# Unit products chained through PSUM, more output rows by seven products, and an order played from a timetable, in a float32 kernel of attention and gated FFN

## The chip, the cores and the metric

The kernel runs on one core of one Trainium2 chip. The time is device microseconds of that core, the median of several runs; a profiled execution gives the rows that are read here.

## The reference

Input x is 2048 x 512. Two branches are mixed row by row with a gate from x:

```python
def reference(A_x, A_wqkv, A_wo, B_x, B_w_gate, B_w_up, B_w_down, gate_w):
    x = A_x
    g = sigmoid((x * gate_w).sum(-1, keepdims=True))
    # A: linear attention, 32 heads of 16, phi(t) = where(t > 0, t + 1, exp(t)) + 1e-6
    q, k, v = heads(x @ A_wqkv)                      # 512 x 1536
    kv = einsum("bhsd,bhse->bhde", phi(k), v); z = phi(k).sum(s)
    a = (phi(q) @ kv / (phi(q) . z + 1e-6)) @ A_wo   # 512 x 512
    # B: bilinear FFN, F = 1792
    b = ((x @ B_w_gate) * (x @ B_w_up)) @ B_w_down   # 512 x 1792, 1792 x 512
    return g * a + (1 - g) * b
```

## The kernel before

Every product is made in float32 as three matmuls of rounded parts: a matrix is split into a high part (a ScalarE copy that rounds) and a low part (a VectorE subtraction), and high x high, high x low and low x high are added in PSUM (`mm3`). A matmul is 128 x 128 weights by 512 columns.

**Phase 1** (`xop`, `k_mm`, `g_unit`) goes over 16 tiles of 128 rows: k = x W_k, phi of it, and the sums g = phi(k)^T x in four PSUM banks (`accs`); the tile's matmuls of k run up to four tiles ahead of those of g. Beside it x is loaded and added in blocks for the units (`cb_load`, `x_add`), and the raw weights of the first units come in.

**Phase 2** goes twice (a pair of 512-row chunks each time, `pair` 0 and 1) through 16 units: 14 of the FFN (gate and up columns of one block f of 128) and two of attention (q columns). `order` lists the 32 units. A **unit** is a 2 x 2 block product (two weight columns by two row chunks, inner dimension halved) done with seven products of six matmuls instead of eight; x sums and weight sums go in, and PSUM banks Y, X, R, S collect them. Before, the sums between products go through VectorE: `m2` is a ScalarE copy of Y, R = X - m2, t = R + cross0, S = t - X, and at the end the two multiplications of gate by up (`hidden`).

The raw weights of a unit (`wr`, seven blocks of 128 KB in two buffers) come as a load of three blocks on SP's queue, two ScalarE copies and one accumulating transfer of five blocks on GpSimd's queue (`w_load`, `w_add`); `w_high` and `w_low` split them into `wch` and `wcl` (two buffers).

**Down jobs** turn the units' results into output rows. A plain pair of rows is `down_jobs`: eight jobs of two rows, one PSUM bank each (`pdn`). `seven` does groups of pairs by seven products over four banks (`sa`, `sb`), with weights made of loads and accumulating transfers (`ws`, from `in_wdn`, `wrow` and their negatives `dminus`, `wminus`). Twelve of the 18 row pairs are done so, in groups of two: FIRST_SEVEN (four pairs in the first half) and SEVEN (eight in the second).

The order of everything is written by hand: `later(n, place, fn)` hangs work at a place of a unit, `do` runs it, FIRST and SECOND say after which product how many down jobs follow (`down`), and `advance` starts ScalarE, VectorE and weight steps of jobs ahead by leads. Buffers of phase 2 are 58 slots of 128 x 512 (`Buf`, `NS`). All engines and queues keep program order (`pin`). Output of the first half goes out on GpSimd's queue, of the second on SP's.

Of the kernel before, what the change touches and what calls it, by code (L numbers as in the profile page):

```python
# [31 lines left out]
LEAD_X = 4  # L32
LEAD_W = 17
GAP_L = 6
GAP_A = 14
HB = 8
FIRST_SEVEN = (((4, 5), (6, 7)), (('a', 0), (8, 9)))
FIRST_AT = (4, 8)
MINUS_AT = (1, 2, 3)
XAT = (11, 6, 4, 8, 11, 7, 11, 13, 13, 13, 10, 13)  # L40
WUNIT = (8, 5, 2)
FIRST = (
    (3, 1, 3, 0), (0, 3, 2, 1), (0, 0, 1, 1), (2, 0, 1, 0), (0, 1, 0, 2), (0, 0, 0, 1), (1, 2, 0, 2), (0, 3, 0, 0),
    (0, 0, 2, 2), (0, 2, 3, 1), (2, 1, 1, 1), (3, 2, 0, 2), (2, 0, 1, 0), (3, 3, 3, 3), (1, 2, 0, 0), (3, 0, 2, 3),
)
PLACES = "high low e m c d t s r end".split()
ATT = ((0, 8, 5, 4, 6, 4, 5, 3), (0, 5, 12, 5, 0, 9, 4, 13))
NS = 58
SECOND = (
    (2, 1, 1, 0), (0, 0, 1, 3), (2, 1, 0, 3), (1, 0, 0, 0), (0, 1, 0, 2), (0, 0, 1, 2), (2, 0, 0, 2), (0, 2, 0, 1),  # L50
    (0, 2, 1, 2), (2, 2, 2, 0), (0, 0, 2, 1), (0, 3, 3, 1), (0, 3, 1, 0), (2, 2, 0, 1), (3, 0, 2, 3), (3, 1, 0, 2),
)
STARTS = (0, 4, 4, 10)
MOST = (2, 2, 2, 2)
MOST_0 = (1, 1, 2, 2)
LEAD_X0 = 4
LEADS_0 = (15, 7, 12)
RELOAD = ((0, 1), (0, 2), (3, 4), (5, 6))
Q_AFTER = ((5, 9), (0, 3))

SLOT = {3: 0, 4: 1, 2: 2, 5: 3, 1: 4, 6: 5, 7: 6}
# [3 lines left out]
def gated_mix(ctx: ExitStack, tc, xt, xp, x, wqkv, wq, wq_add, wo, wgu, wgu_add, wdn, gate_w, out):  # L71
# [39 lines left out]
    def dma_add(dst, src):  # L111
# [17 lines left out]
    own = {i: [const.tile([P, 2, CH], F32R, name=f"xc{i}{v}") for v in "hl"] for i in (1, 4, 6)}  # L129
    xc = {2: [v[:, 0:2] for v in xa], 7: [v[:, 2:4] for v in xa],  # L130
          3: [v[:, 0:2] for v in xb], 5: [v[:, 2:4] for v in xb], **own}


    zeros = own[1][0][:, 0, 0:CH // 2].bitcast(mybir.dt.bfloat16)
# [9 lines left out]
    xsum = {i: dram.tile([P, 2, CH], F32, name=f"xsum{i}") for i in (1, 5, 6, 7)}  # L144
# [28 lines left out]
    def w_add(n):  # L173

        if n < len(order):
            _, kind, m = order[n]
# [4 lines left out]
    PARTS = ((0, 2), (2, 4), (4, 7))  # L181
# [7 lines left out]
    def w_low(n, part):  # L189
        if n < len(order):  # L190
# [5 lines left out]
    SUMS = {1: (A1, B2, 0), 3: (B1, B2, 1), 4: (A2, A1, 1), 6: (A1, B1, 0), 7: (A2, B2, 0), 2: (None, A1, 0),  # L196
            5: (None, B2, 0)}

    def x_load(tile_, pair, i, ks):
        dma(tile_, xp[pair, SUMS[i][1]][:, ks])  # L200

    def x_add(tile_, pair, i, ks):
        one, _, sub = SUMS[i]
        if sub:
            act(tile_, tile_, scale=-1.0)
        if one is not None:
            dma_add(tile_, xp[pair, one][:, ks])
# [4 lines left out]
    with tc.tile_pool(name="p1", bufs=2, reuse_waits="tile") as p1:  # L212

        warm = psum.tile([P, CH], F32, tag="Y", name="warm")
        for _ in range(WARM):
            mm(warm, zeros[:, :P], zeros, start=True, stop=True)
        gw = p1.tile([P, D], F32, name="gw", bufs=1)
        zacc = p1.tile([P, D], F32, name="zacc", bufs=1)
        nc.vector.memset(zacc, 0.0)
        wkh = p1.tile([P, KT, D], F32R, name="wkh", bufs=1)  # L220
# [7 lines left out]

        raw_of = [p1.tile([P, D], F32, tag="raw", name="wraw", bufs=4) for _ in range(KT)]
# [39 lines left out]
        def phi_k(t, pk):  # L269

            e = p1.tile([P, D], F32, tag="e", name="e")
            r = p1.tile([P, D], F32, tag="u", name="r")
            act(e, pk, AF.Exp)
            act(r, pk, AF.Relu)
            ph = p1.tile([P, D], F32, tag="ph", name="ph")
            stt(ph, e, 1.0, r, ALU.min, ALU.add)
            return t, ph

        def phi_split(t, ph):
            pkh = p1.tile([P, D], F32R, tag="pkh", name="pkh", bufs=4)  # L280
            pkl = p1.tile([P, D], F32R, tag="pkl", name="pkl", bufs=4)
            act(pkh, ph, AF.Identity, bias=epsc)
            stt(pkl, ph, EPS, pkh.bitcast(F32), ALU.add, ALU.subtract)
            stt(zacc, ph, EPS, zacc, ALU.add, ALU.add)
            pks[t] = (pkh, pkl)

        def split_x(t):
            raw = xs.pop(t)
            xnh = p1.tile([P, D], F32R, tag="xnh", name="xnh")
            xnl = p1.tile([P, D], F32R, tag="xnl", name="xnl")  # L290
            split(xnh, xnl, raw)
            junk = p1.tile([P, D], F32, tag="junk", name="junk", bufs=1)
# [47 lines left out]
        def cb_load(i):  # L340
            cbs[i] = p1.tile([P, 2, CH], F32, tag="cbs", name="cbs", bufs=3)
            x_load(cbs[i], 0, i, slice(0, 2))

        for t, i in zip((6, 7, 9, 10, 12), (4, 1, 6, 7, 3)):
            plan(t, lambda i=i: cb_load(i))
            plan(t + 2, lambda i=i: x_add(cbs[i], 0, i, slice(0, 2)))
            plan(t + 5, lambda i=i: split(*xc[i], cbs.pop(i)))
        for n, t in ((0, 8), (1, 11)):
            plan(t, lambda n=n: w_load(n))
            plan(t + 2, lambda n=n: w_add(n))  # L350
        plan(14, lambda: w_high(0))
        for part in range(3):
            plan(14 + part // 2, lambda part=part: w_low(0, part))
        plan(16, lambda: w_load(2))
# [36 lines left out]
    p2 = ctx.enter_context(tc.tile_pool(name="p2", bufs=1, reuse_waits="tile"))  # L391
    live = []
    spare, kept = [], {}

    class Buf:

        def __init__(self, name, rounded=False):
            self.home = rounded and bool(spare)
            one = spare.pop(0) if self.home else p2.tile([P, CH], F32R if rounded else F32, tag="s", name=name, bufs=NS)
            self.f = one.bitcast(F32) if rounded else one  # L400
            self.r = one
            if not self.home:
                live.append(self)
                assert len(live) <= NS, clock[0]

    def put(*some):
        for one in some:
            if one.home:
                spare.append(one.r)
            else:  # L410
                live.remove(one)

    def two(name):
        return [Buf(name + v, True) for v in "hl"]

    def split_buf(name, src, copy="act"):

        hi, lo = two(name)
        split(hi.r, lo.r, src, copy)
        return hi, lo  # L420


    at = {}

    def later(n, place, fn):
        at.setdefault((n, place), []).append(fn)

    def do(n, place):
        for fn in at.pop((n, place), []):
            fn()  # L430
        clock[0] += 1
        most = MOST if n >= units else MOST_0
        advance(dve=most[0], act=most[1])


    jobs, clock = [], [0]

    class Job:

        def __init__(self, mms, chains=(), after=None, apart=0, group=None, first=False):  # L440
            self.first, self.mms, self.after, self.apart, self.group = first, mms, after, apart, group
            self.chains = [list(c) for c in chains]
            self.free = [0] * len(self.chains)

    def always():
        return True

    def advance(**most):

        for i, job in enumerate(jobs):  # L450
            for k, chain in enumerate(job.chains):
                while chain:
                    kind, lead, gap, fn, ready = chain[0]
                    if lead < i or clock[0] < job.free[k] or not ready() or not most.get(kind, 1):
                        break
                    if kind in most:
                        most[kind] -= 1
                    fn()
                    job.free[k] = clock[0] + gap
                    chain.pop(0)  # L460

    owed, passed, running = [0], [0, 0], [None]

    def down(k, all_=False):

        owed[0] += k
        for _ in range(owed[0]):
            if not jobs or passed[0] - passed[1] < jobs[0].apart and not all_:
                break
            waits = [stage for chain in jobs[0].chains for stage in chain]  # L470
            if waits and not all_:
                break
            for kind, lead, gap, fn, ready in waits:
                assert ready(), clock
                fn()
# [8 lines left out]
            if job.after:  # L484
                job.after()
# [761 lines left out]
```

## Time and profile before

| what | value |
|---|---|
| median of 3 runs | 591.1 us (590.35 to 592.35) |
| profiled execution, span from first to last instruction | 591.5 us |
| TensorE busy | 583.7 us, 2610 matmuls |
| VectorE, ScalarE, GpSimd busy | 491.3, 364.9, 100.3 us |
| DMA | 106.19 MB, 180 GB/s over the span |

The profile gives no device time of its own for that execution beyond the span; the span is 0.4 us above the median of the runs. In the profile's rows PE is TensorE, PEld its weight loads, DVE VectorE, ACT ScalarE, POOL GpSimd and SP the queue that issues plain loads; `out<-in` are the program's names without buffer numbers; the number behind a bar is idle time of the engine just before these instructions and what ended it. L79, L85 and L88 are lines of helpers (matmul, activation, tensor_tensor), so names tell more than lines.

### The profile page before, as it was taken

The numbers are of one execution on the slowest core, as the hardware profiler recorded it, in microseconds if no ns is written. First come the engines' busy times: TensorE is split into PE (matmuls) and PEld (weight loads), VectorE is DVE, ScalarE is ACT, GpSimd is POOL, SyncE is SP. The second block draws the span as 40 slices with busy tenths as digits, with TensorE's granted clock in tenths as the row PEclk, the third lists the DMA queues.
The fourth block names the chain that finished last, engine by engine and source line by source line (L and its number), as shares of the span: only waits on it lengthen the run. The fifth ranks groups of instructions, "written<-read, shape, count | busy, mean of one in ns | idle before, by whom it ended". The sixth has DMA issues, their size and how long they took to land.

```text
span 591.5 us, 7915 instructions
## 1 busy us (share of the span) xinstructions
PE 583.7 (99%) x2610; PEld 478.0 (81%) x2610; DVE 491.3 (83%) x798; ACT 364.9 (62%) x649; POOL 100.3 (17%) x123
## 2 busy tenths in 40 slices
PE   9999999999999999999999999999999999999997
PEld 6888888888888868788888788888888888888886
DVE  6877895775567889999869967998798999799987
ACT  3856774677647475688456747458956846646520
POOL 0011100000151124111020042305010322301000
PEclk9999999999999999999999999999999999999999
DMA  9476946868898879556798699779875676834003
GB/s 296 168 201 129 284 106 197 213 194 225 252 225 205 204 211 208 146 120 161 213 239 248 211 221 224 226 155 244 215 168 133 176 148 148 186 71 63 0 2 142
DMA packets 68249, 106.19 MB, mean 180 GB/s; under 512 B 8864, under 2 KB 40352, under 8 KB 68192
## 3 DMA queue, kind: packets, MB, share of 16 engines
q1 hardware_dynamic: 51872, 68.98, 35.5%
q0 software_dynamic: 16048, 36.18, 34.9%
q10 hardware_dynamic: 288, 0.52, 0.3%
q8 instruction: 20, 0.33, 0.2%
q14 instruction: 21, 0.17, 0.1%
HBM read 90.70 MB, written 15.61 MB: 180 GB/s over the span
## 4 chain that ended last, share of the span: by engine, by line
PE 90%; DVE 5%; issue 2%; DMA 2%; ACT 1%; POOL 0%; DVEq 0%; POOLq 0%; ACTq 0%
PE bY L79 13%; PE bX L79 13%; PE bR L79 13%; PE sa L79 11%; PE pdn L79 9%; PE sb L79 8%; PE pk L79 8%; PE gt L79 7%; PE bS L79 7%; DMA wr<-in_wgu_add 2%; DVE wcl L88 1%; DVE acc L88 1%; PE warm L79 1%; PE pw L79 0%; DVE cross L88 0%
## 5 line engine op out<-in xcount | busy, mean ns | idle before, releaser
L88 DVE TENSOR_TENSOR wcl<-wr,wch 128x512 fp32r<-128x512 f32 (+1 forms) x96 | 73.2, 772 | 2.0 <-ACT wch L85 1.9
L85 ACT ACTIVATE wch<-wr 128x512 fp32r<-128x512 f32 (+1 forms) x96 | 60.3, 691 | 4.9 <-DMA wr<-in_wgu_add 4.6
L112 POOL DMA_DIRECT2D wr<-in_wgu_add x28 | 25.0, 892 | 207.7 <-ACT wr L85 153.4
L79 PE MATMUL bX<-xbh,wch 128*128 128x512 f32 x128 | 47.3, 390 | 0.0
L79 PE MATMUL bX<-xbl,wch 128*128 128x512 f32 x128 | 47.2, 389 | 0.0
L79 PE MATMUL bX<-xbh,wcl 128*128 128x512 f32 x112 | 43.6, 389 | 0.0
L85 ACT ACTIVATE cross<-bY 128x512 f32<-128x512 f32 x32 | 19.0, 594 | 33.4 <-PE bY L79 33.3
L88 DVE TENSOR_TENSOR bR<-bX,m 128x512 f32<-128x512 f32 x32 | 22.2, 695 | 20.5 <-PE bX L79 19.6
L85 ACT ACTIVATE m<-bY 128x512 f32<-128x512 f32 x32 | 19.0, 593 | 31.7 <-PE bY L79 31.7
L112 POOL DMA_DIRECT2D ws<-dminus x27 | 31.1, 1341 | 35.7 <-DVE wl L88 24.7
L85 ACT ACTIVATE wr<-wr 128x512 f32<-128x512 f32 x64 | 36.4, 618 | 0.3 <-DMA wr<-in_wgu 0.3
L85 ACT ACTIVATE xh<-cross 128x512 fp32r<-128x512 f32 x38 | 23.5, 626 | 20.7 <-DVE cross L88 19.7
L88 DVE TENSOR_TENSOR t<-bR,cross 128x512 f32<-128x512 f32 x32 | 22.0, 687 | 15.0 <-PE bR L79 6.9
L88 DVE TENSOR_TENSOR acc<-pdn,acc 128x512 f32<-128x512 f32 (+1 forms) x39 | 25.4, 671 | 8.1 <-PE pdn L79 7.9
L85 ACT ACTIVATE cross<-bX 128x512 f32<-128x512 f32 x32 | 19.0, 593 | 21.3 <-DVE bS L88 21.2
L79 PEld LDWEIGHTS bX<-xbh,wch 128*128 128x128 f32 x128 | 24.0, 188 | 5.3 <-ACT cross L85 0.3
L79 PEld LDWEIGHTS bX<-xbl,wch 128*128 128x128 f32 x128 | 24.0, 188 | 5.0
L88 DVE TENSOR_TENSOR xl<-cross,xh 128x512 fp32r<-128x512 f32 x38 | 25.9, 684 | 2.4 <-ACT xh L85 2.2
L79 PE MATMUL bS<-xah,wch 128*128 128x512 f32 x64 | 25.1, 392 | 0.7 <-DVE bS L88 0.7
L112 POOL DMA_DIRECT2D ws<-in_wdn x18 | 24.1, 1721 | 9.1 <-DMA ws<-in_wdn 9.1
L79 PE MATMUL pdn<-hl,dh 128*128 128x512 f32 (+1 forms) x65 | 25.2, 388 | 0.0
L79 PE MATMUL pdn<-hh,dl 128*128 128x512 f32 (+1 forms) x65 | 25.1, 386 | 0.0
(310 smaller groups left out, 1823.6 us busy)
## 6 DMA issues: line engine op xcount, KB each, us to landing
wr<-in_wgu_add POOLq DMA_DIRECT2D x28, 640.0 KB, 6.9
wr<-in_wgu SPq DMA_DIRECT2D x28, 384.0 KB
ws<-in_wdn SPq DMA_DIRECT2D x45, 128.0 KB
xraw<-in_x SPq DMA_DIRECT2D x16, 256.0 KB
terms<-zq SPq DMA_DIRECT2D x16, 256.0 KB
zt<-terms SPq DMA_DIRECT2D x16, 256.0 KB
rb<-den SPq DMA_DIRECT2D x16, 256.0 KB
ws<-dminus POOLq DMA_DIRECT2D x27, 128.0 KB, 4.8
```

The source lines that it names most:

```text
L79: tc.keep_in_program_order(nc.tensor.matmul(*args, **kw))
L85: pin(nc.scalar.activation(dst, src, func, **kw))
L88: pin(nc.vector.tensor_tensor(dst, a, b, op=op))
L112: tc.keep_in_program_order(nc.gpsimd.dma_start(dst, src, accum_op=ALU.add))
```

## The change

Phase 2 is written anew; phase 1 keeps its matmuls.

- Units: the seven products are chained. Product 1 fills Y, ScalarE copies Y into PSUM bank R, product 6 adds onto R; S = R + m5 with m5 a ScalarE copy of X (product 5); product 7 adds onto R, and cross1 = R + m5; products 3 and 4 add onto S and R.
- Raw weights: the load has other blocks, and the one add of five blocks becomes three adds of one, one and two blocks, each behind the one before and a ScalarE copy; three buffers instead of two.
- Output rows: 16 of 18 pairs by seven products, eight in each half, in groups of three, three, two and two, three, three (LINE); one plain pair first and one last. For a pair there are nine small transfers of weights (five loads, four adds) instead of eleven (six and five); a third pair in a group has weight roundings of its own at half width. Step 6 has a new ScalarE copy of raw weights.
- x sums: A1, A2 and B2 are used as they are (products 1, 2, 3), the others come from two chains of negations and adds.
- Order: all operations of phase 2 are first listed as Op objects with cost and dependences; `run` plays them on five engines and two DMA queues, and the instructions are written out in the order in which the play started them. A transfer's consumers are let go SPARE = 3.5 us after its played landing. TensorE picks between the stream of units ("u") and of down jobs ("j"); SHARE says how many jobs are due after each 14 products. Steps that take a buffer wait until AHEAD us before they are due.
- Output of both halves goes out on SP's queue. The pool has 54 slots instead of 58. Some tiles of phase 1 are allocated in another sequence (`early`).

The diff, cut to its core:

```diff
-FIRST_SEVEN = (((4, 5), (6, 7)), (('a', 0), (8, 9)))
...
-NS = 58
+NS = 54
+NR = 3
+LANES = 8
+LINE = (
+    (0, ((0, 1),)),
+    (0, ((2, 3), (4, 5), (6, 7))),
+    (0, (('a', 0), (8, 9), (10, 11))),
+    (0, ((12, 13), ('a', 1))),
+    (1, ((0, 1), (2, 3))),
+    (1, (('a', 0), (4, 5), (6, 7))),
+    (1, (('a', 1), (8, 9), (10, 11))),
+    (1, ((12, 13),)),
+)
+SHARE = (0.0, 2.5, 6.5, 10.5, 13.4, 19.5, 28.8, 37.0, 45.2, 53.5, 62.7, 71.9, 80.2, 89.4, 98.8, 109.2, 122.0)
+AHEAD = {"load": 20.0, "act": 9.0, "dve": 8.0, "back": 59.0}
+SPARE = 3.5
+X_AT = (6, 8, 13, 7, 9, 11, 14, 16)
+W_AT = ((7, 9, 10, 11), (10, 12, 13, 14))
...
-            raws[n] = const.tile([P, 7, 2 * P], F32, tag="wr", name="wr", bufs=2)
+            raws[n] = const.tile([P, 7, 2 * P], F32, tag="wr", name="wr", bufs=NR)
...
-            act(raws[n][:, 3:5], raws[n][:, 0:1].to_broadcast([P, 2, 2 * P]))
-            act(raws[n][:, 5:7], raws[n][:, 0:2], scale=-1.0)
-            dma_add(raws[n][:, 2:7], (wgu_add if kind == "f" else wq_add)[m])
+                act(raw[:, 3:4], raw[:, 2:3])
+                dma_add(raw[:, 3:4], more[:, 0:1], 0.72)
+                act(raw[:, 4:5], raw[:, 3:4], scale=-1.0)
+                dma_add(raw[:, 4:5], more[:, 1:2], 0.72)
+                act(raw[:, 5:7], raw[:, 4:5].to_broadcast([P, 2, 2 * P]))
+                dma_add(raw[:, 5:7], more[:, 2:4], 1.41)
...
+            product(1, "Y", True)
+            act(bk["R"], bk["Y"])
+            product(5, "X", True)
+            m5 = Buf("m5")
+            act(m5.f, bk["X"])
+            product(6, "R")
+            tt(bk["S"], bk["R"], m5.f, ALU.add)
+            product(2, "Y")
+            act(cross[0].f, bk["Y"], scale=-1.0 if turned[0] else 1.0)
...
+            product(7, "R")
...
+                tt(cross[1].f, bk["R"], m5.f, ALU.add)
...
+            product(3, "S")
...
+                tt(cross[1].f, bk["S"], cross[1].f, ALU.mult)
+            product(4, "R")
...
+            tt(cross[0].f, bk["R"], cross[0].f, ALU.mult)
...
+                elif step == 6:
+                    five = Buf("ws")
+                    for of, add in (((0, 1), False), ((1, 1), True)):
+                        for i in chunk:
+                            if add:
+                                dma_add(half(five, i), block(i, *of), 0.72)
+                            else:
+                                dma(half(five, i), block(i, *of), 0.42)
+                    src = Buf("ws")
+                    act(src.f[:, 0:n], five.f[:, 0:n])
...
+            def may(op, t):
+                if op.work and late[op] - t > CALM and flow[0] > QUEUE:
+                    again(t + 0.5, op.engine)
+                    return False
...
+                if engine == "PE":
+                    some = [heads[s][at[s]] for s in "uj" if at[s] < len(heads[s])]
+                    if len(some) == 2 and at["j"] < share(at["u"]):
+                        some.reverse()
+                    for op in some:
+                        if open_[op] and may(op, t):
+                            return take(op, t)
+                    return
+                for _, _, op in ready[engine]:
+                    if may(op, t):
+                        return take(op, t)
...
+                        push(t + OUT[e], "land", q[2])
+                        push(t + OUT[e] + SPARE, "sure", q[2])
...
+            for op in line:
+                for node in op.nodes:
+                    if node.real is None:
+                        node.real = place[node].get() if node in place else node.make()
+                op.fn()
```

More of the change, by code (lines that the diff above doesn't have):

```diff
@@ L142, in gated_mix @@
                             pattern=[[DH, P // DH], [0, DH]], channel_multiplier=-1)
-    xsum = {i: dram.tile([P, 2, CH], F32, name=f"xsum{i}") for i in (1, 5, 6, 7)}
+    xsum = {i: dram.tile([P, 2, CH], F32, name=f"xsum{i}") for i in (4, 5, 6, 7) if i not in KEPT}
     grow = dram.tile([2, NT, P], F32, name="grow")
@@ L406, in put @@
[L406 to L433, printed above, removed]
@@ L436, in gated_mix @@
[L436 to L460, printed above, removed]
@@ L462, in gated_mix @@
[L462 to L475, printed above, removed]
-            job = jobs.pop(0)
-            running[0] = job.group
-            owed[0] -= 1
-            clock[0] += 1
-            job.mms()
-            passed[1] = passed[0]
-            most = MOST_0 if job.first else MOST
-            advance(dve=most[2], act=most[3])
-            if job.after:
-                job.after()
-        if not jobs:
-            owed[0] = 0
@@ new lines, in mix, with finished @@
+        outs = fixed(out, (D, S))
+        acc, left = {}, {(pair, i): len(of_pair[pair]) for pair in range(NPAIR) for i in range(TPP)}
+        tags = ["dn", "att"]
+        def finished(pair, i, cols, gated):
+            c, d = divmod(i, KT)
+            a = acc[pair, i].f[:, cols]
+            if not gated:
+                tt(a, a, og[pair, c].f[:, cols], ALU.mult)
+            t = (pair * 2 + c) * CH
+            dma(outs[d * P:(d + 1) * P, t + cols.start:t + cols.stop], a, 0.59 * (cols.stop - cols.start) / CH)
@@ L746, in mms, with plain @@
+        def plain(pair, key):
+            one = scheme[pair, key]
+            ends = pair and key == of_pair[1][-1][0]
+            for i in [(i + TPP // 2) % TPP for i in range(TPP)]:
+                c, d = divmod(i, KT)
+                sl = slice(d * P, (d + 1) * P)
                 step = CH // 2 if ends and i == TPP // 2 - 1 else CH
@@ L1143, in plain @@
-    def plain(n):
-        return order[n][1] == "f" and (order[n][0], order[n][2]) not in row_of
-    ffn = [n for n in range(len(order)) if plain(n)]
-    def d_load(i):
-        if i < len(ffn):
-            n = ffn[i]
-            wdr[n] = Buf("wdr")
-            dma(wdr[n].f, wdn[order[n][2]])
-    d_load(0)
-    wp_load()
-    g_evac()
-    d_load(1)
-    rows = []
-    for some, place in SEVEN:
-        later(units + place, "end", lambda some=some: jobs.extend(
-            seven(1, [fps[1, key] for key in some], some == SEVEN[-1][0])))
@@ L1195, in gated_mix @@
-    down(len(jobs), True)
+                    tags.reverse()
+                    pd = bank(tags[0], "pdn")
+                    some = []
+                    for r in range(2):
+                        some += mm3(pd[:, cols], [v.r[:, sl] for v in one["rows"][r]],
+                                    [v.r[:, cols] for v in one["b"][r, c]], r == 0, r == 1, late=1)
+                    pe("j", some)
+                    to_acc(pair, i, pd, cols, o + step == CH)
+        STEPS = (1, 6, 2, 7, 5, 4, 3)
@@ L1198 @@
+        for pair, some in LINE:
+            if len(some) == 1:
+                plain(pair, some[0])
+            else:
+                seven(pair, some)
+        plan(todo_ops, units)
+    mix()
 def kernel(A_x, A_wqkv, A_wo, B_x, B_w_gate, B_w_up, B_w_down, gate_w):
```

1436 lines of the change are left out of this document (788 added, 648 removed).

## The prediction

> **What bounds the kernel now.** I read the page's busy times first, then the table of stages, the waits of TensorE, the chain that ended last, and last the groups of instructions and the transfers.
>
> ```profile
> span 591.5 us, 7915 instructions
> ...
> PE 583.7 (99%) x2610; PEld 478.0 (81%) x2610; DVE 491.3 (83%) x798; ACT 364.9 (62%) x649; POOL 100.3 (17%) x123
> ...
> PEclk9999999999999999999999999999999999999999
> ```
>
> ```profile
> core 0: us, PE busy (x) PEld busy (x) DVE busy (x) ACT busy (x) POOL busy (x), PEclk, DMA share, GB/s
> ...
> 5.00:93.00 88.00, 88.00 (x385) 72.88 (x386) 73.05 (x135) 55.65 (x95) 6.27 (x7) 1.00 0.70 192
> 93.00:205.00 112.00, 112.00 (x550) 92.68 (x549) 75.34 (x119) 71.40 (x131) 18.94 (x22) 1.00 0.85 220
> 205.00:345.00 140.00, 137.30 (x596) 110.54 (x595) 125.77 (x199) 91.06 (x161) 22.84 (x26) 1.00 0.77 196
> 345.00:580.00 235.00, 235.00 (x1038) 194.32 (x1037) 207.74 (x330) 144.83 (x260) 51.19 (x61) 1.00 0.63 145
> 580.00:591.50 11.50, 7.80 (x41) 6.51 (x39) 8.06 (x14) 0.00 (x0) 0.00 (x0) 0.95 0.48 182
> ```
>
> TensorE is busy in every stage and at full clock; VectorE has a sixth of its time free, ScalarE and the transfers more. The only idle stretch between start and tail is 2.7 us in 205 to 345. The waits say who ended it:
>
> ```profile
> PE sb L79 <- ACT xh L85: 1.1, 1, 1.1
> PE sa L79 <- ACT xh L85: 0.7, 1, 0.7
> PE bS L79 <- DVE bS L88: 0.7, 1, 0.7
> ```
>
> So time is counted in matmuls. The chain gives the price of one:
>
> ```profile
> 4.95 14.63 PE pk L79 x60
> ...
> 27.75 2.72 PE pk L79 x12
> ...
> 106.62 2.02 PE pkv L79 x64
> ...
> 579.80 8.02 PE pdn L79 x41
> ```
>
> A 512-column matmul takes 2.72 / 12 = 0.2267 us. The busy time is not the sum of these: a matmul's row is 0.39 us long and covers short gaps. I therefore counted again. Of 2610 matmuls 8 are the warm-up, 64 the small ones of pkv (2.02 us) and 12 the 256-column ones at the end (some 0.12 us each, 1.4 us together); the other 2526 need 572.6 us, in all 576.1 us. From 4.95 to the end of the chain's last TensorE piece at 587.8 are 582.9 us. So 6.8 us are lost between matmuls: 14.63 - 13.60 = 1.0 in the first sixty, and about 5.7 inside, of which the waits show 2.5. Around the largest of them:
>
> ```profile
> 212.07 0.39 PE L79 MATMUL sb<-xl,wh 128*128 128x512 f32 x1
> 213.58 0.50 PE L79 MATMUL sb<-xh,wh 128*128 128x512 f32 x1 [1.12 <-ACT xh L85]
> ```
>
> 1.51 us from start to start instead of 0.23. (The Trainium skill, "Trainium Kernel Development and Optimization", section Performance Expectations, says that matmul busy time is a bad measure of how near a kernel is to its limit, since matmuls are pipelined. The trace agrees: by busy time the best possible gain would stop at 2.5 us of stalls, by spacing at 5.7.)
>
> **The change part by part.**
>
> Products. A pair of output rows done plainly is 8 jobs x 2 rows x 3 = 48 matmuls; by seven products it is 7 x 2 x 3 = 42. Seven-product pairs go from 12 (4 and 8) to 16 of 18 (8 and 8): 4 x 6 = 24 matmuls fewer, 2586 in all. 24 x 0.2267 = 5.44 us off the engine that sets the end. A unit still has seven products of six matmuls; pkv, pw, phase 1's matmuls and the halved last job stay.
>
> The units' chain. VectorE's work per unit falls from five to four operations between PSUM and SBUF (S, cross1 and two multiplications; the old R, t, S and the same two), ScalarE's three copies stay three.
>
> ```profile
> L88 DVE TENSOR_TENSOR bR<-bX,m 128x512 f32<-128x512 f32 x32 | 22.2, 695 | 20.5 <-PE bX L79 19.6
> ...
> L88 DVE TENSOR_TENSOR t<-bR,cross 128x512 f32<-128x512 f32 x32 | 22.0, 687 | 15.0 <-PE bR L79 6.9
> ```
>
> That frees 32 x 0.69 = 22 us of VectorE, off the path. What the chain adds on the path are tight places: product 6 adds onto R, into which ScalarE has just copied Y, with only product 5 (1.36 us) between; product 7 adds onto R, which VectorE has just read, with only product 2 between; product 4 the same behind product 3. The kernel before lives with such a place already:
>
> ```profile
> 99.86 0.70 DVE L88 TENSOR_TENSOR bS<-t,bX 128x512 f32<-128x512 f32 x1 [0.61 <-PE bX L79]
> ...
> 101.02 0.39 PE L79 MATMUL bS<-xah,wch 128*128 128x512 f32 x1
> ```
>
> Here S was written at 100.56 and used at 101.02 behind one product: 0.46 us to spare, and in 32 units it failed once by 0.7. I take 0; above, bound as in rival 2; below 0 nothing, since the copies were never waited for in 93 to 205.
>
> Four more pairs by seven. Plain, a pair costs ScalarE 6 roundings and VectorE 14 operations; by seven it costs 7 and 11, plus seven roundings of weights on each engine per two pairs (a third pair in a group has its own, at half width), plus 12 VectorE and 6 ScalarE operations per group, and there are six groups before and after.
>
> ```profile
> L85 ACT ACTIVATE xh<-cross 128x512 fp32r<-128x512 f32 x38 | 23.5, 626 | 20.7 <-DVE cross L88 19.7 <-DMA xsum<-cb 0.9
> ...
> L85 ACT ACTIVATE minus<-wdr 128x256 f32<-128x256 f32 x6 | 2.3, 405 | 0.0
> ...
> L88 DVE TENSOR_TENSOR xl<-cross,xh 128x512 fp32r<-128x512 f32 x38 | 25.9, 684 | 2.4 <-ACT xh L85 2.2
> ```
>
> VectorE: 44 x 0.68 + 28 half ones x 0.41 - 56 x 0.68 = +3.6 us. ScalarE: 28 x 0.63 + 28 x 0.41 + ten new copies of weights (5.4) - 24 x 0.63 = +19; the third copy per raw-weight buffer adds 0.41 + 0.41 + 0.62 against 2 x 0.62, +6 over 30 units. So VectorE goes from 83% to about 81%, ScalarE from 62% to about 67%: no new bound; on the path 0.
>
> Raw weights. One add of 640 KB per unit becomes three in a row (128, 128, 256 KB), each waiting for the one before and a ScalarE copy; a third buffer gives it more time.
>
> ```profile
> wr<-in_wgu_add POOLq DMA_DIRECT2D x28, 640.0 KB, 6.9
> ...
> ws<-dminus POOLq DMA_DIRECT2D x27, 128.0 KB, 4.8
> ...
> cb<-in_xp POOLq DMA_DIRECT2D x10, 256.0 KB, 6.4
> ws<-in_wdn POOLq DMA_DIRECT2D x18, 128.0 KB, 6.6
> out<-acc POOLq DMA_DIRECT2D x8, 256.0 KB, 4.1
> ```
>
> Load 4.1 to 6.9 (the 384 KB one has no landing; the ends are the lightest and heaviest rows), copies 0.41 + 0.41 + 0.62, adds 4.8 to 6.6 twice and 6.4, splits 0.83 + 0.62 + 0.62 + 0.68: 24 to 31 us. A buffer is free from the middle of a unit until two and a half units later. How long that is:
>
> ```profile
> 94.42 0.60 ACT L85 ACTIVATE m<-bY 128x512 f32<-128x512 f32 x1 [0.76 <-PE bY L79]
> ...
> 198.79 0.58 ACT L85 ACTIVATE m<-bY 128x512 f32<-128x512 f32 x1
> ...
> L85 ACT ACTIVATE m<-bY x32: 579/598/616, 94.4 to 562.3; 128x512 f32<-128x512 f32 x32
> ```
>
> The first eight units took 13.0 us each, all 31 steps 15.1 on average. The new list of shares puts only 13.4 jobs beside the first 56 products: (56 + 13.4) x 1.36 / 8 = 11.8 us per unit, so 29.5 us for the chain there, and about 39 later (some 15.7 per unit). It fits by the low end and misses by 1.5 us at the high end, in the first eight units alone, where the first three buffers are filled ahead. I take 0: later units have 8 us and more to spare. (The Trainium skill, "DMA: Bandwidth & Descriptors", section Anatomy of one DMA, gives a DMA on this path about 2.0 us of fixed cost plus bytes at 436 GB/s and so speaks for one large transfer against three small; as an estimate by that page the three are 7.2 us against 3.5, the chain is far shorter than by the rows and the sum stays. The measured 4.8 to 6.9 are twice its figures and decide.)
>
> GpSimd's queue. Its transfers go from 115 to 172: 96 adds of raw weights for 32, 64 of down weights for 60, 12 for x against 15, no stores of output for 8.
>
> ```profile
> L112 POOL DMA_DIRECT2D wr<-in_wgu_add x28 | 25.0, 892 | 207.7 <-ACT wr L85 153.4
> ...
> L112 POOL DMA_DIRECT2D ws<-in_wdn x18 | 24.1, 1721 | 9.1 <-DMA ws<-in_wdn 9.1
> ...
> L777 POOL DMA_DIRECT2D out<-acc x8 | 4.5, 562 | 27.6 <-DVE acc L88 27.6
> ```
>
> At 0.56 to 1.72 us each that is 96 to 296 us of 586, no bound by itself; but adds queue behind each other, +1 to +4 us in a chain. The eight stores move to SP, where each waits at the head for VectorE with weight loads behind it (27.6 us in eight waits on GpSimd before); an order played with times puts them near when they are ready, so 0, at worst a late load as in rival 1. Bytes added by transfer fall from 36.2 to 29.4 MB; the DMA share falls with them.
>
> Phase 1: x sums need four splits instead of five; the raw weights' adds stand one tile apart (24 x 0.2267 = 5.44 us) while one needs 0.41 + 4.8 to 6.6. ScalarE will wait up to 1.6 us there, four times; it works 55.65 of 88 us and TensorE runs on tiles split ahead, so 0, at most +2. Four buffers fewer in the pool (54): 0; if short, SP's waits on VectorE grow, as in rival 1.
>
> The order. All engines' queues follow one played timetable that treats a transfer as 3.5 us later than it plays it. The 5.7 us of interior stalls may go to 0 or double. I keep 5.7: the old stalls hang on ScalarE and VectorE queues, not on a cause the change takes away by name. Start (4.95) and tail (591.5 - 587.8 = 3.7) stay.
>
> Sum: 591.5 - 5.4 = 586.1 of span. The median of the runs, 591.1, is 0.4 below the profiled span, so 585.7.
>
> **The rivals.**
>
> 1. Slower: the chain of three adds comes late. GpSimd's queue adds 2 x 1.7 us to the high end: 31 + 3.4 = 34 us against 29.5, 1.8 us per unit. From unit 4 to 8 that is 7 us; the ScalarE copy that waits for an add holds the PSUM copies behind it, so TensorE stands. 585.7 + 7 = 593, and up to 600 if later units miss too. It decides once 5.4 us are lost (chain over 33 us). For it: DMA share 0.85 in 93 to 205, and the 153 us in which GpSimd's add waits for ScalarE's copy today. Against: fewer bytes, head start, 39 us later.
>
> 2. No change: the tight places. If VectorE or ScalarE is inside a 0.95 us operation when its turn comes, TensorE loses up to 0.95 - 0.46 = 0.5 us. 0.17 us in each of 32 units makes 5.4 and gives 591.1. Against: the same cover held in 93 to 205 with 0 idle.
>
> 3. Better: the played order takes the old stalls away as well: 585.7 - 5.7 = 580 at the limit, 582.5 when half go.
>
> **How the numbers follow.** Forecast, stalls within about 2.5 us of today's: 583.3 to 588.3, 0.60. Rival 3, below 583.3: 0.10. Stalls grown by 2.5 to 3.6 us, 588.3 to 589.3: 0.08. Rival 2 and mild lateness, 589.3 to 592.9: 0.11. Rival 1, above: 0.11. The range reaches from 582 to 591: it leaves out about 0.04 below and 0.16 above. 0.3% of 591.1 is 1.8 us, about what a measurement of this kernel can tell from no change: faster 0.78, same 0.11, slower 0.11.
>
> **What would show it.** Right: 2586 matmuls 0.2267 apart; TensorE's waits of 2 to 4 us in all; the tail 3.7 us; VectorE near 475 us, ScalarE near 390. Rival 1: TensorE waits behind ScalarE copies whose own waits end on raw-weight adds, between 130 and 190 us. Rival 2: many waits of 0.1 to 0.5 us of bR and bS on VectorE and ScalarE. Wrong altogether: a clock under full, or a load of down weights on SP behind an output store.

## The result and the profile after

| | before | after |
|---|---|---|
| median | 591.29 us (590.35 to 592.35) | 582.33 us (581.9 to 583.16) |
| ratio | 1 | 0.9844 [0.9828, 0.986] |
| span of the profiled execution | 591.5 us | 580.8 us |
| TensorE lost between matmuls, behind the first sixty | 5.1 us in eight places | 0.2 us |

A ratio is against before, timed beside the kernel in question, with its 95% interval in brackets. Two executions, one of the kernel with 2.0 us of allowance (765.1 us) and one of an old-chain kernel (977.9 us), ran at a mean granted clock of 0.72 and 0.56 and are left out of the medians.

The change takes 9.0 us off, where 5.4 were forecast. "Lost" is counted from start to start: what a matmul of 512 columns begins later than 0.2267 us after the one before it. (The subtraction in the prediction gave 5.7 for before; made the same way for after, it gives 0.24.)

The page of after, its totals, clock, one group and the raw weights' transfers:

```profile
span 580.8 us, 8126 instructions
...
PE 575.1 (99%) x2586; PEld 474.8 (82%) x2586; DVE 470.2 (81%) x781; ACT 387.6 (67%) x726; POOL 152.5 (26%) x180
...
PEclk9999999999999999999999999999999999999999
...
DMA packets 77947, 97.82 MB, mean 168 GB/s; under 512 B 9872, under 2 KB 52112, under 8 KB 77904
...
L524 DVE TENSOR_TENSOR bS<-bR,m 128x512 f32<-128x512 f32 x32 | 22.3, 697 | 13.7 <-PE bR L546 5.7
...
wr<-in_wgu SPq DMA_DIRECT2D x28, 384.0 KB, 5.3
wr<-in_wgu_add POOLq DMA_DIRECT2D x56, 128.0 KB, 4.8
wr<-in_wgu_add POOLq DMA_DIRECT2D x28, 256.0 KB, 5.5
```

There are 2586 matmuls, 24 fewer. VectorE's time fell by 21 us, ScalarE's rose by 23. The raw weights' chain is 5.3 + 4.8 + 4.8 + 5.5 us of landings.

The stages of after (columns as in the table of before):

```profile
93.00:205.00 112.00, 112.00 (x550) 92.81 (x549) 67.94 (x104) 71.33 (x142) 34.91 (x40) 1.00 0.73 167
205.00:345.00 140.00, 140.00 (x619) 116.05 (x618) 124.23 (x206) 110.86 (x211) 46.52 (x53) 1.00 0.93 232
```

In 205 to 345, where before stood for 2.7 us, TensorE now makes 619 matmuls instead of 596, and is never idle. The waits of TensorE in after are these two rows, both before 5.2 us:

```profile
PE warm L77 <- DVE xc5h L133: 1.3, 1, 1.3
PE pk L77 <- ACT wkh L83: 0.3, 1, 0.3
```

And the chain that ended last (start, length, what):

```profile
5.18 14.36 PE pk L77 x60
...
565.79 10.96 PE pdn L546 x54
```

By the prediction's own subtraction: start 4.95 to 5.18 (+0.2), first sixty 14.63 to 14.36 (-0.3), products -5.4, stalls 5.7 to 0.24 (-5.5), tail from the end of the last piece 3.7 to 4.0 (+0.3): -10.7, as the spans say.

The listed times are not spans. In every run the time is 1.7 to 2.0 us above the span (after's profiled execution: 582.53 for 580.8). So before's profiled 591.5 was, as an estimate, a run of some 593.2 us, above its median by 1.9. If that excess is all stalls, a typical run of before lost nearer 3.2 to 3.8 us than 5.1 (19 executions of before beside the later kernels have spans from 588.8 to 591.4, median 590.2). That it is all stalls is not shown: the first sixty matmuls alone take 13.7 to 14.8 us, start to start, in thirteen traces. With 3.5, the middle, 591.29 - 5.44 - 3.5 = 582.35, and 582.33 was measured; that they agree so closely is luck.

What made the old stalls? The two largest were at 212 (2.0 us) and 250 (1.25 us). Before's chain of waits ahead of the first:

```profile
196.71 9.68 DMA wr<-in_wgu_add
...
206.47 0.64 ACT wch L85
...
208.52 0.96 DVE den L1012
...
209.71 0.95 DVE wcl L88
210.66 1.21 DVE cross L88 x2
...
211.89 0.64 ACT xh L85
```

One accumulating transfer took 9.68 us instead of the median 6.9; ScalarE stood 3.9 us for it, VectorE's operations bunched up behind, and the roundings that product `sb` needed came last. The one that released the matmul at 213.58 stands a little further down in ScalarE's queue and ends at 213.53:

```profile
212.91 0.62 ACT L85 ACTIVATE xh<-cross 128x512 fp32r<-128x512 f32 x1
```

At 250 no transfer stands in the rows ahead; VectorE's own turn comes late:

```profile
249.36 0.68 DVE L91 SCALAR_TENSOR_TENSOR rb<-ph,rb 128x512 f32<-128x512 f32 x1
...
250.08 0.63 ACT L85 ACTIVATE xh<-rb 128x512 fp32r<-128x512 f32 x1 [1.01 <-DVE rb L91]
...
250.76 0.50 PE L79 MATMUL sa<-xh,wh 128*128 128x512 f32 x1 [0.70 <-ACT xh L85]
```

The last `rb` step ends at 250.04, and rounding it leads straight into the matmul. The third largest, 0.85 us at 339, is a wait for VectorE's bS. The experiments ask what removed these: fewer products alone, a lighter VectorE, quicker or later-counted transfers, or the order.

### The profile page after: what moved, and what is told of

Read it like the earlier page. It is cut to its first block, busy times and chain, and to the rows that moved or that the text cites. A ratio compares the mean times of both kernels' runs of the same rounds, so it can differ in the third digit from the quotient of the medians.

```text
span 580.8 us, 8126 instructions
## 1 busy us (share of the span) xinstructions
PE 575.1 (99%) x2586; PEld 474.8 (82%) x2586; DVE 470.2 (81%) x781; ACT 387.6 (67%) x726; POOL 152.5 (26%) x180
## 4 chain that ended last, share of the span: by engine, by line
PE 98%; DMA 1%; ACT 0%; DVE 0%; issue 0%
PE bR L546 22%; PE bY L546 15%; PE sa L546 15%; PE sb L546 11%; PE pk L77 8%; PE bX L546 8%; PE gt L77 7%; PE bS L546 7%; PE pdn L546 4%; DMA wraw<-in_wqkv 1%; PE pw L546 0%; PE pkv L546 0%; ACT wkh L83 0%; DVE acc L524 0%
## 5 line engine op out<-in xcount | busy, mean ns | idle before, releaser
L539 POOL DMA_DIRECT2D wr<-in_wgu_add x78 | 74.5, 989 | 199.8 <-ACT wr L517 186.6
L517 ACT ACTIVATE wr<-wr 128x256 f32<-128x256 f32 (+1 forms) x90 | 42.6, 480 | 0.9 <-DMA wr<-in_wgu_add 0.9
L546 PE MATMUL bY<-xah,wcl 128*128 128x512 f32 x96 | 37.4, 390 | 0.0
L546 PE MATMUL bY<-xah,wch 128*128 128x512 f32 x96 | 37.4, 390 | 0.0
L546 PE MATMUL bY<-xal,wch 128*128 128x512 f32 x96 | 37.4, 389 | 0.0
L524 DVE TENSOR_TENSOR bS<-bR,m 128x512 f32<-128x512 f32 x32 | 22.3, 697 | 13.7 <-PE bR L546 5.7
L546 PE MATMUL bX<-xc5h,wch 128*128 128x512 f32 x64 | 25.0, 391 | 0.0
L546 PE MATMUL bX<-xc5h,wcl 128*128 128x512 f32 x64 | 24.9, 390 | 0.0
L546 PE MATMUL bX<-xc5l,wch 128*128 128x512 f32 x64 | 24.9, 390 | 0.0
L77 PE MATMUL gt<-pkh,xnl 128*128 128x512 f32 x64 | 24.9, 390 | 0.0
L546 PE MATMUL bR<-xc7h,wch 128*128 128x512 f32 x64 | 24.9, 390 | 0.0
```

What stands on the lines that cost most here:

```text
L77: tc.keep_in_program_order(nc.tensor.matmul(*args, **kw))
L517: return Op("ACT", lambda: pin(nc.scalar.activation(get(dst), get(src), func, **{k: get(v) for k, v in kw.items()})), c, c + 0.11, [src, * ...
L524: return Op("DVE", lambda: pin(getattr(nc.vector, name)(get(dst), *[get(v) for v in ins], **kw)), c, c + 0.085, some, [dst], kind="dve")
L539: return Op("POOL", lambda: pin(nc.gpsimd.dma_start(get(dst), get(src), accum_op=ALU.add)), 0.54, 0.0, [src, dst], [dst], work=work, kind= ...
L546: tc.keep_in_program_order(nc.tensor.matmul(get(dst), get(lhs), get(rhs), **kw))
```

## The experiments

**Products alone.** After with groups cut so that 12 pairs go by seven, as many as before (six in each half, where before has four and eight).

```diff
-    (0, ((2, 3), (4, 5), (6, 7))),
-    (0, (('a', 0), (8, 9), (10, 11))),
+    (0, ((2, 3), (4, 5))),
+    (0, (('a', 0), (6, 7))),
+    (0, ((8, 9),)),
+    (0, ((10, 11),)),
...
-    (1, (('a', 0), (4, 5), (6, 7))),
-    (1, (('a', 1), (8, 9), (10, 11))),
+    (1, (('a', 0), (4, 5))),
+    (1, (('a', 1), (6, 7))),
+    (1, ((8, 9),)),
+    (1, ((10, 11),)),
```

> The changed kernel with the old number of products: 12 of 18 pairs by seven (four and eight, in groups of two), the six others plain, all else as changed. 24 matmuls more, 2610 as before. If the old stalls went because all queues follow the played timetable (theory A), because VectorE has less to do per unit (B) or because late transfers are allowed for (C): no stalls between matmuls (under 0.7 us), 582.3 + 24 x 0.2267 = 587.8 us, 3.5 us under the kernel before. If they went because more pairs go by seven in larger groups (D): stalls of about 5 us are back, 591 to 593 us.

588.7 us (587.89 to 588.93), ratio 0.995 [0.9936, 0.9965], 2610 matmuls, 0.8 us lost. So 24 matmuls are worth 588.7 - 582.33 = 6.4 us here (5.44 of spacing and 0.6 more stalls; 0.3 are not accounted for), and with the old number of matmuls all the rest of the change together (chain, transfers, order) is still 3.0 us faster than before.

**The allowance for late transfers.** In this and in four more kernels (those with two buffers, an allowance of 2.0, the old chain's first form, and one VectorE operation more) SHARE stands in slightly other numbers and QUEUE at 2 instead of 4. First the three buffers kept and the allowance set to zero.

```diff
-SPARE = 3.5
+SPARE = 0.0
-QUEUE = 4.0
+QUEUE = 2.0
```

> The changed kernel with an allowance of 0 instead of 3.5 us for late transfers, three buffers as changed, shares of the two streams such that the timetable itself waits no more than the changed kernel's. C: stalls of 2 to 5 us, 584 to 587 us. A and B: under 0.7 us, 582 to 583 us. If it is the buffer and not the allowance that matters, this one stays at 582 to 583 while the one with two buffers goes up.

613.59 us (610.8 to 617.89), ratio 1.0371 [1.0311, 1.0431]: slower than before, with the same 2586 matmuls. Waits in that kernel:

```profile
ACT wr L517 <- DMA wr<-in_wgu_add: 38.6, 23, 4.4
...
ACT wr L517 <- DMA wr<-in_wgu: 16.7, 11, 5.3
...
PE bR L546 <- ACT bR L517: 11.4, 5, 6.1
```

In after the first of these rows reads 0.9 us, once. The largest of the TensorE waits can be read off ScalarE's queue (start, length, idle before and its releaser):

```profile
266.67 0.63 ACT L517 ACTIVATE wr<-wr 128x512 f32<-128x512 f32 x1 [2.68 <-DMA wr<-in_wgu_add]
271.76 0.63 ACT L517 ACTIVATE cb<-cb 128x512 f32<-128x512 f32 x1 [4.46 <-DMA cb<-in_xp]
...
275.53 0.57 ACT L517 ACTIVATE bR<-bY 128x512 f32<-128x512 f32 x1
```

Two waits for transfers, 7.1 us together, hold everything behind them, and the copy of Y into R, which product 6 needs, comes after both at 275.53; the matmul waited 6.05 us. This is rival 1's mechanism, though later than rival 1 had put it (130 to 190 us): the first stall of over 1 us ends at 192.67, this largest one at 276.16. It also strikes on x sums (`cb`), not only on raw weights.

Then two buffers with no allowance, and three with 2.0:

```diff
-NS = 54
-NR = 3
+NS = 56
+NR = 2
-SPARE = 3.5
+SPARE = 0.0
```

> The changed kernel with two raw-weight buffers instead of three, a timetable that lets consumers go at a transfer's played landing (allowance 0 instead of 3.5 us; with two buffers none can be played with it) and 56 slots; its timetable itself has no more waits of TensorE than the changed kernel's. C: transfers that land later than played stall TensorE through the three chained adds, 3 us or more, 585 to 592 us. A and B: 582 to 583 us.

605.38 us (604.49 to 608.56), ratio 1.0245 [1.0215, 1.0274].

```profile
ACT wr L517 <- DMA wr<-in_wgu_add: 26.5, 23, 3.9
ACT wr L517 <- DMA wr<-in_wgu: 20.0, 11, 3.7
```

Without the allowance the third buffer brings no gain that shows: two buffers, with 56 slots instead of 54, were quicker than three. Whether two would do with the allowance is open.

```diff
-SPARE = 3.5
+SPARE = 2.0
```

> As the run with allowance 0, same shares, with 2.0 us. C: the loss lies between the 31 us at 0 and nothing at 3.5 us; transfers land up to 3 us apart in the rows (5.8 to 9.8 us for one kind), so part of them is still late: 584 to 592 us. If the 31 us came from the altered shares and not from the allowance: 605 us or more here too.

584.18 us (582.6 to 584.66, three runs), ratio 0.9876 [0.9851, 0.9902]. One wait of TensorE is left inside, and the chain that leads to it starts at a late transfer:

```profile
PE bR L546 <- DVE cross L524: 0.9, 1, 0.9
...
ACT wr L517 <- DMA wr<-in_wgu_add: 13.2, 9, 4.5
...
104.34 6.48 DMA wr<-in_wgu_add
...
115.18 0.96 PE bR L546 x3
```

So 0, 2.0 and 3.5 us of allowance give 613.6, 584.2 and 582.3, and ScalarE's waits for these transfers go from 38.6 to 13.2 and 0.9 us. The altered shares are in the first two alike, so they are not what costs the 29 us between them. The last step, 1.9 us, is not told apart: the runs overlap (582.6 to 584.66 and 581.9 to 583.16), and the shares differ.

**The timetable's costs.** After with VectorE's durations entered at 0.6 of what they are. The work is the same; only the order that the play finds differs.

```diff
-            c = cost or n / 960 + 0.066
+            c = (cost or n / 960 + 0.066) * 0.6
```

> The changed kernel with one wrong price in its timetable: VectorE's operations are played at 0.6 of their cost, nothing else. If the gain needs an order played with the chip's own durations (A in its strong form): stalls of 5 us or more, 588 us or above. If any list ordered by need will do (A in its weak form) or the allowance for transfers covers it as well (C): under 2 us, 582 to 584.5 us.

603.98 us (603.75 to 607.68), ratio 1.0235 [1.0204, 1.0267].

```profile
PE bR L546 <- DVE bS L524: 7.2, 4, 3.1
```

The same chain, products, buffers and allowance, with one wrong price in the play: 21.6 us lost, some 6 of them in matmuls at half clock behind the stalls (last section). It shows what a bad order costs; it does not show that the order by hand made the old stalls. The tight place of rival 2 (R read by VectorE for S, then filled by product 7) is where it shows.

**The chain and VectorE's load.** After with the old unit chain (R and S through VectorE):

```diff
-            act(bk["R"], bk["Y"])
+            m2 = Buf("m2")
+            act(m2.f, bk["Y"])
             product(5, "X", True)
-            m5 = Buf("m5")
-            act(m5.f, bk["X"])
-            product(6, "R")
-            tt(bk["S"], bk["R"], m5.f, ALU.add)
+            tt(bk["R"], bk["X"], m2.f, ALU.subtract)
...
+            product(6, "R")
+            t = Buf("t")
+            tt(t.f, bk["R"], cross[0].f, ALU.subtract if turned[0] else ALU.add)
+            product(7, "X")
+            tt(bk["S"], t.f, bk["X"], ALU.subtract)
+            act(cross[1].f, bk["X"], scale=-1.0 if turned[1] else 1.0)
```

> The changed kernel with the units' old pattern of waits and VectorE work: m2 copied to SBUF, R = X - m2, t = R + cross0, S = t - X, two multiplications (five VectorE operations per unit for four), the timetable played anew for it. The products' inputs stay those of the new scheme, so the unit sums that come out are not those of the reference; the work is that of the old chain. A and C: stalls stay under 0.7 us, 582 to 583 us, VectorE about 22 us busier. B: stalls of 3 to 5 us come back, 585 to 587.5 us.

585.7 us, ratio 0.9903 [0.9888, 0.9918], 3.1 us lost, 2.0 of them in six losses of some 0.33 us at the same place of a unit (the next expectation says seven):

```profile
100.24 0.60 ACT L517 ACTIVATE cross<-bX 128x512 f32<-128x512 f32 x1 [2.06 <-PE bX L546]
...
100.87 0.69 DVE L524 TENSOR_TENSOR bS<-t,bX 128x512 f32<-128x512 f32 x1 [1.23 <-ACT cross L517]
...
101.62 0.50 PE L546 MATMUL bS<-xbh,wch 128*128 128x512 f32 x1
```

VectorE's S waits until ScalarE has read the same bank X, though neither writes it. The rows show a semaphore that ScalarE's read raises; whether the chip or the program asks for it they do not show. The play does not know of that, so it cost 0.33 us where it struck. To take this fault of the experiment away, ScalarE's read was listed behind S and the shares of after put back:

```diff
-            tt(bk["S"], t.f, bk["X"], ALU.subtract)
-            act(cross[1].f, bk["X"], scale=-1.0 if turned[1] else 1.0)
+            first_read = tt(bk["S"], t.f, bk["X"], ALU.subtract)
+            act(cross[1].f, bk["X"], scale=-1.0 if turned[1] else 1.0).after.add(first_read)
```

> The old chain of the units once more (its results again not those of the reference, the work that of the old chain), now with ScalarE's copy of bank X listed behind VectorE's S = t - X, as in the kernel before; all parameters as in the changed kernel. In the first run of the old chain seven units lost 0.32 us at S, each behind a ScalarE read of the same bank which the timetable did not know to hold VectorE off. Theory A and C (the order, not VectorE's load): those go, stalls under 1 us, 582 to 583.3 us with VectorE still some 20 us busier. B (VectorE's load itself): stalls of 2 to 4 us stay, 584.5 to 586.5 us.

584.68 us over three runs, ratio 0.9893 [0.9877, 0.991]. The only trace is that of the 977.9 us, so the same kernel was profiled again:

> The second old-chain kernel once more, unchanged (old chain of the units, ScalarE's read of bank X behind VectorE's), since the profile of its first run shows a throttled clock throughout and cannot be read; its three other runs gave 584.7 us. VectorE's load (B): stalls of about 2.5 us between matmuls, spread over stages where VectorE is fullest. The chain's pattern of waits: the same sum, at one and the same product of the units (bS or bR) in the units without jobs beside them.

584.74 us, ratio 0.9883 [0.9861, 0.9905], 3.5 us lost, no longer at one place of the units, and 1.0 of them at 88 us, in phase 1:

```profile
PE bS L546 <- DVE xbl L524: 1.3, 1, 1.3
...
PE gt L77 <- DVE xnl L86: 0.7, 1, 0.7
PE bS L546 <- DVE bS L524: 0.2, 1, 0.2
```

The old chain in the new order, with shares that were set for the new chain, is 2.4 us slower than after. Is that VectorE's load or the pattern? After with one VectorE operation more in each unit, that nothing waits for:

```diff
+            more = Buf("more")
+            tt(more.f, m5.f, m5.f, ALU.add)
```

> The changed kernel with one more VectorE operation per unit that nothing waits for (m5 + m5 into a buffer of its own), so VectorE has the old amount of work per unit but the new chain; timetable played with it. B (load): 584 to 585.5 us, as the old chain. Chain's pattern: 582 to 583 us, stalls under 0.7 us.

583.33 us (582.54 to 583.72), ratio 0.9855 [0.9834, 0.9877]. The page:

```profile
PE 575.8 (99%) x2586; PEld 473.8 (81%) x2586; DVE 488.4 (84%) x813; ACT 385.2 (66%) x726; POOL 152.5 (26%) x180
```

VectorE is as busy as with the old chain (489.7 us) and the kernel is 1.0 us slower than after by medians, with intervals that overlap; 1.2 of the 1.6 us lost lie at 86 to 88 us, the end of phase 1. The old chain's times lay where VectorE's load (B) was to put them, but this kernel, with the same load, came out between its two cases (582 to 583 and 584 to 585.5). So VectorE's load is worth at most about 1 us. The other 1.4 us can lie in the old chain's waits or in shares that do not suit it; the runs do not separate these. Read the other way, new order and transfers with the old chain win 591.95 - 584.74 = 7.2 us, 5.4 of them by matmuls: 1.8 us of the 3.5, and the new chain has a part in the rest.

**The same causes in before.** First the raw weights' transfer cut from five blocks to one (the other four blocks are left as the copies made them):

```diff
-            dma_add(raws[n][:, 2:7], (wgu_add if kind == "f" else wq_add)[m])
+            dma_add(raws[n][:, 2:3], (wgu_add if kind == "f" else wq_add)[m][:, 0:1])
```

> The kernel before with a raw-weight add of one block (128 KB) instead of five (640 KB); the other four blocks keep their copies, so its unit products are not those of the reference. C (late transfers make the old stalls): the stalls at about 107 and 212 us go, 0.2 and up to 2 us, 589 to 590.5 us against 591.2. A (order of ScalarE and VectorE): the stalls at 250, 293, 298, 328 and 339 us stay, 3 us, and the time falls by under 1 us.

590.7 us (589.68 to 590.92) against 591.95, ratio 0.9978 [0.9967, 0.999].

```profile
PE sa L79 <- ACT xh L85: 0.7, 1, 0.7
PE sb L79 <- DVE xl L88: 0.2, 1, 0.2
```

The wait of 1.1 us of `sb` is gone, of the 2.0 us at 212 only 0.8 are left, and of the 0.85 us at 339 only 0.2; the one at 250 is as it was. Then VectorE's t operation taken out:

```diff
-        t = Buf("t")
-        tt(t.f, bank["R"], cross[0].f, ALU.subtract if turned[0] else ALU.add)
...
-        tt(bank["S"], t.f, bank["X"], ALU.subtract)
-        put(t)
+        tt(bank["S"], cross[0].f, bank["X"], ALU.subtract)
```

> The kernel before without t = R + cross0 (S = cross0 - X instead), one VectorE operation per unit fewer, 22 us in all; its results are not those of the reference. B (VectorE's load): most of the interior stalls go, 587.5 to 588.5 us. A (a fixed order): under 1 us of change, 590.2 to 591.2 us, stalls at the same places.

589.84 us (589.11 to 590.44), ratio 0.9964 [0.9953, 0.9974]. TensorE's largest wait is again the one at 250:

```profile
PE sa L79 <- ACT xh L85: 0.7, 1, 0.7
```

VectorE has 18 us less work, the small stalls at 293 and 298 go, 0.45 us are left at 212 and 0.3 at 339, 250 stays. By medians the reliefs take off 1.2 and 2.1 us; in the traces both shrink the same two stalls, by 1.2 to 1.5 us at 212 and 0.5 to 0.7 at 339. The second is no clean test at 212: in its trace the transfer that had taken 9.68 us took 8.14, and ScalarE waited 2.40 us for it instead of 3.93:

```profile
204.26 1.37 ACT L85 ACTIVATE wch<-wr 128x512 fp32r<-128x512 f32 x2 [2.40 <-DMA wr<-in_wgu_add]
```

It also shortens the chain of waits, besides VectorE's load. Both times lie between the cases that were expected. The stall at 250 needs neither; the order written by hand is what is left to explain it, and no run of before with another order shows it.

**One pair more.** After with 17 of 18 pairs by seven, and shares and four limits of the play set for it:

```diff
-    (0, ((0, 1),)),
-    (0, ((2, 3), (4, 5), (6, 7))),
-    (0, (('a', 0), (8, 9), (10, 11))),
-    (0, ((12, 13), ('a', 1))),
+    (0, ((0, 1), (2, 3))),
+    (0, ((4, 5), (6, 7))),
+    (0, (('a', 0), (8, 9))),
+    (0, ((10, 11), (12, 13), ('a', 1))),
```

> A version meant to beat both: the first plain pair goes by seven too (17 of 18 pairs; first half in groups of two, two, two, three), shares and four waiting rules of the timetable chosen anew so that it plays without waits. Six matmuls fewer, 6 x 0.2267 = 1.36 us. If matmuls still set the time: 580.9 us. If the early units, which then have no jobs beside them for longer, run ahead of their raw weights: 582.5 to 585 us.

581.5 us (581.22 to 582.03), ratio 0.9841 [0.9827, 0.9856], span 579.9. By medians it is the fastest of all, 0.8 us under after where six matmuls make 1.36; the interval overlaps after's, so it is not told apart from after.

## Why the prediction was right or wrong

The measured 582.33 us lies in the range of 582 to 591, but at its low edge, below 583.3, in the band that was given to rival 3. The range holds the number because it reached down to rival 3, not because the forecast had the stalls right.

**Products: right.** 24 matmuls at 0.2267 us, 5.44 us; 2586 in the trace, and 6.4 us between 12 and 16 pairs.

**Stalls: the term that was mis-sized.** "I keep 5.7: the old stalls hang on ScalarE and VectorE queues, not on a cause the change takes away by name." Yet the change replaces both the order of those queues and the chain that feeds them. Measured: 0.2 us left, and of the waits of 2 to 4 us that were to show the forecast right, 0.3 us behind the warm-up. The case I had named with a chance of 0.10 (the played order takes the old stalls away) is the one that came. What the runs show: with the old number of products the new kernel is still 3.0 us faster; with the old chain in the new order some 2.4 us come back; with a wrong duration in the play it is 21.6 us slower; lighter VectorE or shorter adds in the old order take away 2.1 and 1.2 us. How the 3.5 us divide between order and chain stays open. What I should have weighed: an operation that stands 0.2 to 1.25 us too late in a queue is what a play with durations can see and move, and VectorE and ScalarE had the free time for it.

**Span to median: wrong by about 2 us.** I put the median 0.4 below the profiled span; by the runs a time is 1.7 to 2.0 above its span, so the profiled execution must have been among the longest. So all stalls gone came out where rival 3 had put half of them gone (582.5, with 580 for all). The two errors partly cancel: had the stalls stayed as they typically are, 591.29 - 5.44 = 585.85 would have come. The miss of 3.4 us is the stalls term.

**Units' chain, 0: right.** After has no wait on bR or bS at all. The dangers were real: with VectorE's price wrong they cost 7.2 us in four waits.

**Three adds in a row, 0: right, but for a reason I under-weighted.** The landings sum as in the low end of my 24 to 31 us, and the first eight units took 11.9 us each where I had 11.8. Yet without the allowance the same chain, buffers and transfers cost 31 us more, by rival 1's mechanism. I argued from the mean room (29.5 us against the chain); what decides is how early the ScalarE copy stands in its queue against when the transfer lands in a bad case, such as 9.68 us for a median of 6.9 in before, or 8.6 for 5.1 among the raw weights' adds of after. (The Trainium skill, "DMA: Bandwidth & Descriptors", section Anatomy of one DMA, would make 2.3 us of a 128 KB transfer, as an estimate from its 2.0 us and 436 GB/s; the trace has 4.8.)

**Third buffer.** Taken as what makes the chain fit. The runs do not show that: with no allowance two buffers (and two more slots) beat three.

**VectorE, ScalarE, phase 1: right.** 470 us where I had "near 475", 388 for "near 390". (The terms of VectorE's +3.6 us add up to +3.3; nothing rests on it.) Phase 1's late adds made ScalarE wait more than I said, and it cost nothing in after:

```profile
ACT wr L83 <- DMA wr<-in_wgu_add: 6.8, 2, 4.6
```

**Open.** The stalls of 0.3 to 1 us at 86 to 88 us, the end of phase 1, come in four of the variants (with one VectorE operation more, with the old chain, two buffers, and wrong VectorE costs) and not in after. Phase 1's work is the same in all; why they come was not settled. Nor was after run with the altered shares and 3.5 us.

## What to carry to other kernels

When an order by hand is replaced by a played one, take the stalls of the old order as a term that can go to nearly zero where the engines behind them have free time, and look for what the play cannot know: how late a transfer may land, and dependences that it does not list. A consumer in an in-order queue should be placed for the late landing, not for the typical one; here 2.0 us of allowance were worth 29 us. And before a sum is made against one profiled execution, find out where that execution stands among its runs.

## What the hardware showed that was not expected

A gap of TensorE can cost more than its length. In the kernel with wrong VectorE costs two starts lie 3.45 us apart, the second at 354.37; stages of that kernel:

```profile
345.00:350.00 5.00, 5.00 (x23) 4.13 (x22) 5.00 (x9) 2.97 (x6) 0.00 (x0) 1.00 0.89 145
352.00:355.00 3.00, 0.63 (x2) 0.53 (x3) 3.00 (x6) 2.46 (x5) 0.71 (x1) 0.75 0.00 0
355.00:360.00 5.00, 5.00 (x13) 3.94 (x12) 4.83 (x9) 4.25 (x8) 0.15 (x1) 0.50 0.69 173
360.00:365.00 5.00, 5.00 (x23) 4.08 (x22) 3.36 (x5) 2.93 (x6) 2.98 (x4) 0.96 0.90 194
```

Behind the gap the granted clock is 0.50, and in 5 us stand 13 matmuls instead of 23. Where two starts lie 2.81 us apart, the second at 407.47, matmuls keep their pace for 0.9 us and then start 0.43 us apart for about 3 us:

```profile
407.47 0.50 PE L546 MATMUL bR<-xc7h,wch 128*128 128x512 f32 x1 [2.42 <-DVE bS L524]
...
408.36 0.63 PE L546 MATMUL bR<-xc7h,wch 128*128 128x512 f32 x1
408.79 0.63 PE L546 MATMUL bR<-xc7l,wch 128*128 128x512 f32 x1
...
411.68 0.40 PE L546 MATMUL bS<-xh,wcl 128*128 128x512 f32 x1
```

A start every 0.43 us instead of 0.2267 for some 3 to 6 us loses 1.5 to 2.9 us more. In the kernel without allowance such starts add up to some 7 of its 31 us. The length of the gap alone does not decide it. By the clock records of the traces, in the kernels without allowance, with two buffers and with wrong VectorE costs, starts 2.53, 2.56, 2.81 and 3.36 us apart were followed by a clock of 0.50 for 3.41 us, those 3.45, 4.02 and 6.44 us apart by 6.83 us of it, while behind starts 2.66 and 2.93 us apart, and behind shorter ones that stood alone, it stayed full; two of 1.4 us close behind each other (at 465 us with wrong VectorE costs) brought it down too. (The Trainium skill, "TensorE: Matmul & The Clock Gate", Part 1, says that the clock is halved after an idle window of about 3.4 us that runs freely. The trace agrees on the half; gaps shorter than 3.4 us brought it here in some places and not in others.) In before and after, where matmuls behind the start were never more than 1.51 us apart, the clock stayed full up to the last matmuls.

VectorE's read of a PSUM bank was held until ScalarE's read of it had ended (the old chain's X, some 0.33 us in six units, by a semaphore), and a time was 1.7 to 2.0 us above its span in every run.
